# A scan layer on one core: transforms factored 64 by 32 in place of 32 by 64, in eight TensorE tiles at once

## The chip, the core and the metric

The kernel runs on one core of a Trainium2 chip. A core has a matrix engine (TensorE, PE in the profile, whose weight loads stand apart as PEld), three engines for elementwise work (VectorE or DVE, ScalarE or ACT, GpSimd or POOL), and a sync engine (SyncE, SP), which in this kernel only issues DMA transfers. Each engine works through its own list of instructions in order and waits on semaphores for the others. The metric is the device time in microseconds of one execution; three runs of the kernel before gave 559.74, 561.16 and 561.18 us, and the median, 561.16 us, is the time to beat.

## The reference

One sequence of L = 2048 positions with D = 512 channels goes through two branches of the same normalised input, and the result is `x + s * g`:

```
xn = layernorm(x)
dt = exp(log_dt);  logdA = dt * (A_re + i A_im);  dB = dt * B
K[d, l] = real( sum_n C[d,n] * exp(logdA[d,n] * l) * dB[d,n] )     # n: 128 states
y = irfft( rfft(xn, 2L) * rfft(K, 2L) )[:L]                         # per channel
s = y + xn * Dskip
g = silu( gelu(xn @ w1 + b1) @ w2 + b2 )                            # 512 -> 1792 -> 512
out = x + s * g
```

So `s` is a causal convolution of every channel with its own kernel K of 2048 taps, and K has to be computed from the state-space parameters. All is float32.

## The kernel before, in words

The work falls into three stretches of time.

**0 to about 388 us.** Layernorm, the feed-forward branch (each float32 product as three matmuls of a fast format on high and low halves) and the generation of K run together. Their order is written out by hand as a list of tokens, `ORDER`; each token calls one small function. K is generated in 32 pieces (`gen_sum`, L656) and stored to a DRAM buffer `kgd`, 8 pieces for each of the 4 batches of 128 channels (`gen_keep`, L666).

**About 388 to 406 us, the front.** The last matmuls of the feed-forward branch (tokens S and L, `second_part`) alternate with the first transform of batch 0 (`first_dft`, L864). SyncE meanwhile issues the loads of K for batches 0 and 1 (`kernel_load`, L848) and of two tables (`mc` and `tcn`, `table_load`, L798).

**From 406 us on, the batches.** The convolution is done by a transform in factors. The 2048 positions are split as n = N2 n1 + n2, with N1 = 32 and N2 = 64. For each batch, and for K and the signal alike:

- `first_dft` (L864) transforms over n1. Its stationary operand is a group of 32 rows of the data by 128 columns, and its moving operand the table `fc`, 64 columns for real and imaginary parts. 32 such matmuls fill four PSUM banks, each bank from one group of 32 rows, so four of them stand in the array at once. A batch needs four such calls. `first_out` (L870) copies each bank into `X`.
- `second_dft` (L883) applies the twiddle factors and transforms over n2, from the table `mc`, which is stationary in tiles of 64 rows by 64 columns. Real and imaginary parts are two matmuls that accumulate. 32 matmuls fill two banks.
- `spectrum` (L891, ACT) copies the half that belongs to the signal, `product` (L900, DVE) multiplies, and `combine` (L910 and L912, DVE) adds the products into `Y`. Here the sums move between partitions: each is done in two operations on 64 partitions, and its result is laid so that `Y` has 128 rows for the next transform.
- `back_dft` (L918) transforms back over the second factor, with `Y` stationary (128 by 128) and `tcn` moving; `back_out` (L930, ACT) copies into `Z`.
- `swings` (L936, copies L944) transposes `Z` in four quarters; `last_dft` (L975) transforms back over n1 in tiles of 64 rows by 32 columns with 512 moving columns. `last_out` (L982 and L983) multiplies by the gate and adds x, and `store` (L992) writes out. Of the last batch, two quarters go through `rows_out` instead (L1009), whose matmuls have 128 rows.

The order of this part is that of the calls in `slot(b, g)`: a batch b has eight slots g, each with one call of `second_dft`; the even slots also hold a call of `first_dft` for batch b+1, the odd ones a piece of `back_dft` of this batch or the last piece of the batch before, and the transposes and last transforms of batch b-1 stand in between. Two PSUM banks of `second_dft` are double-buffered (tag "ri"); all the other results go round a ring of four banks (`bank`, L804). After the last slot follow the rest of batch 3 and the last stores, from about 540 us.

In the trace one float32 matmul of the program is four records, two weight loads and two matmuls: 1,024 calls at L883 show as 2,048 records of PE and 2,048 of PEld. A transpose, and a matmul of the fast format, is one of each.

Of the kernel before, what the change touches and what calls it, by code (L numbers as in the profile page):

```python
# [25 lines left out]
N1, N2 = 32, 64  # L26
NB = 4
DB = P // NB
# [8 lines left out]
NPH = N1 + N2 // 2  # L37
NPC = 6
NSEED = 11
NREC = 2 + NSEED  # L40
TWO_PI = 6.2831850
# [50 lines left out]
S.28.0 WS.12.0 F.30.1 KL.18.0 E.15.0 WS.12.1 A.17.0 U.13 D S.28.1 F.31.0 KL.17.1 E.15.1 N.16.0 E.15.2  # L92
# [38 lines left out]
def _shape_constants():  # L131
# [3 lines left out]
    cf = np.tile(np.stack([np.cos(a), -np.sin(a)], 1), (G, 1, 1))  # L135
    cg = np.zeros((2, N1, 2, 3, N1))
    for hh in range(2):
        for c, v in enumerate((np.cos(a).T, -np.sin(a).T)):
            cg[hh, :, c, 0] = v
            cg[hh, :, c, 1:].reshape(N1, N1, 2)[:, :, hh] = v  # L140
    cg = cg.reshape(P, 3 * N1)
    n2 = np.arange(N2)[:, None]
    k2 = np.arange(N2)[None, :]
    cm = np.zeros((2, N2, N1, 3, N2))
    ct = np.zeros((2, N2, N1, 2, N2))
    for k in range(N1):
        th = 2 * np.pi * (n2 * (k + 0.25) / L + n2 * k2 / N2)
        c, s = np.cos(th), np.sin(th)
        cm[:, :, k, 0, :] = c
        cm[:, :, k, 1, :] = s  # L150
        cm[:, :, k, 2, :] = -s
        ct[0, :, k, 0, :] = c.T / L
        ct[1, :, k, 0, :] = -s.T / L
        ct[0, :, k, 1, :] = s.T / L
        ct[1, :, k, 1, :] = c.T / L
    ct = ct.reshape(P, N1, 2, 2, 2, 16).transpose(0, 1, 4, 5, 3, 2)
    cb = np.zeros((CH, NPC, CH, NPH))
    for d in range(CH):
        cb[d, :3, d, :N1] = N2 * np.arange(N1)
        cb[d, :3, d, N1:] = np.arange(N2 // 2) + 0.5  # L160
        cb[d, 3:, d, :N1] = 1.0
# [3 lines left out]
        "cg": cg.astype(f),  # L165
        "cm": cm.reshape(P, N1 * 3 * N2).astype(f),
        "ct": ct.reshape(P, N1 * P).astype(f),
# [5 lines left out]
def kernel(  # L173
# [7 lines left out]
    x_t = u[0].rearrange("(n h j t a q) d -> t h a j n q d", n=N1, h=2, j=2, t=2, a=2)  # L181
    o_l = out[0].rearrange("(r j q) d -> j r q d", j=2, q=NQ)
    o_t = out[0].rearrange("(n h j t a q) d -> t h a j n q d", n=N1, h=2, j=2, t=2, a=2)
# [11 lines left out]
    kgd = [dram.tile([P, DB * N2], F32, name=f"kgd{b}") for b in range(NB)]  # L195
# [8 lines left out]
    dsk = keep.tile([P, NB, DB], F32, name="dsk")  # L204
    GP.memset(dsk, 0.0)
    b1s = keep.tile([P, NF], F32, name="b1s")
    fc = keep.tile([P, 2 * N1], F32, name="fc")
# [277 lines left out]
    def params(b):  # L485
# [61 lines left out]
        V.scalar_tensor_tensor(xp[:, 1], ai, (N2 - 1) / 2.0, an, op0=ALU.mult, op1=ALU.add)  # L547
# [63 lines left out]
    def gen_size(s):  # L611
        rc = gen[s]["rc"]
        mm = par.tile([P, CH, N2 + N1], F32, tag="mm", name=f"mm{s}", bufs=2)
        mv = mm.rearrange("p c (j l) -> p c j l", l=N1)
# [5 lines left out]
        GP.tensor_mul(mm[:, :, N1:N2], mm[:, :, 0:N1], rc[:, 12, :].unsqueeze(2).to_broadcast([P, CH, N1]))  # L620
# [10 lines left out]
    def gen_tables(s, n):  # L631
        ra, mm = gen[s]["ra"], gen[s]["mm"]
        m1, m2 = mm[:, :, N2:], mm[:, :, :N2]
        H = N2 // 2
        up = slice(N1, N1 + H)
        dn = slice(N1 + H - 1, N1 - 1, -1)
        if n == 0:
            e1 = par.tile([P, 2, CH, N1], F32, tag="e1", name=f"e1_{s}", bufs=2)
            e2 = par.tile([P, 2, CH, N2], F32, tag="e2", name=f"e2_{s}", bufs=2)
            gen[s]["e"] = (e1, e2)  # L640
            V.tensor_mul(e1, m1.unsqueeze(1).to_broadcast([P, 2, CH, N1]), ra[:, :, :, :N1])  # L641
            return
# [7 lines left out]
    def gen_sum(s):  # L650
        e1, e2 = gen[s]["e"]
        p = pss.tile([P, DD, N2], F32, tag="sm", name=f"kg{s}")
        for d in range(DD):
            for c in range(2):
                for g in range(G):
                    PE.matmul(p[g * N1:(g + 1) * N1, d, :], e1[:, c, g * DD + d, :], e2[:, c, g * DD + d, :],  # L656
                              start=(c == 0), stop=(c == 1), skip_group_check=True)
        gen[s]["p"] = p

    def gen_out(s):  # L660
        gen[s]["ko"] = ko = par.tile([P, DD, N2], F32, tag="ko", name=f"ko{s}", bufs=2)
        A.copy(ko, gen[s]["p"])

    def gen_keep(s):
        b, j = divmod(s, SPB)
        SY.dma_start(kgd[b][:, j * DD * N2:(j + 1) * DD * N2], gen.pop(s)["ko"].rearrange("p a b -> p (a b)"))  # L666
# [62 lines left out]
    def skip_load():  # L729
        for g in range(G):  # L730
            SY.dma_start(dsk[g * N1:g * N1 + 1], dskip.rearrange("(o b g d) -> g o b d", o=1, b=NB, g=G)[g])
        SY.dma_start(fc, cf)

# [38 lines left out]
        "D": skip_load,  # L772
# [10 lines left out]
    def open_front():  # L783
        SB["pf"] = pf = opened(p2, "pf", "right")
        SB["mc"] = pf.tile([P, N1, 3, N2], F32, name="mc")
        SB["psa"] = opened(p2, "psa", "right", bufs=2, space=PSUM)

    def open_mid():
        SB["pm"] = pm = opened(p2, "pm", "right")
        SB["ps"] = opened(pz, "psm", "left", bufs=2, space=PSUM)  # L790
        SB["tcn"] = pm.tile([P, N1, P], F32, name="tcn")
        SB["gc"] = pm.tile([P, N1], F32, name="gc")

    def table_load(t, src):
        w = t.shape[2] if len(t.shape) == 3 else t.shape[2] * t.shape[3]
        for k in range(0, N1, 8):
            d = t[:, k:k + 8]
            SY.dma_start(d.rearrange("p k m -> p (k m)") if len(t.shape) == 3 else d.rearrange("p k a m -> p (k a m)"),  # L798
                         src[:, k * w:(k + 8) * w])
# [12 lines left out]

# [4 lines left out]
    def side_piece(b, g):  # L817
        t = side.setdefault(b, SB.get("raw1"))
        SY.dma_start(t[g * N1:(g + 1) * N1], xs.rearrange("(n m) (b g d) -> b g n m d", n=N1, b=NB, g=G)[b, g])

    def side_load(b):
# [5 lines left out]
        for g in range(G):  # L827
            side_piece(b, g)
# [346 lines left out]
```

## Time and profile before

| what | value |
|---|---|
| median of three runs | 561.16 us (559.74 to 561.18) |
| span of the profiled execution, first to last instruction | 558.0 us |
| granted TensorE clock, mean | 0.998 |
| PE busy | 540.2 us, 97% (7,179 matmul records) |
| PEld busy | 432.1 us, 77% (7,179 records) |
| DVE busy | 454.2 us, 81% (697 instructions) |
| ACT busy | 407.8 us, 73% (602) |
| POOL busy | 296.3 us, 53% (403) |
| DMA | 86.92 MB, mean 156 GB/s |
| instructions in all | 17,143 |

The profiled execution has no run time of its own beside its span; the span lies 3.2 us under the median of the runs, and the profile's shares are shares of the span. PE is busy nearly throughout, and so its share alone does not tell which stretch is bound by what: matmuls are pipelined, their records overlap, and a record is busy from its start to its modelled end. For the stretches it is more useful to see how far apart groups of records start. The table of queues in the profile also lists the transfers that bring the engines' own instructions from memory, as kind "instruction".

### The profile page before, as it was taken

The page shows a single profiled execution, that of the slowest core. Times are in us where ns is not written, and L with a number is a line of the kernel's source. Part 1 is how long each engine was busy: PE and PEld are TensorE (multiplying, and loading weights), DVE is VectorE, ACT ScalarE, POOL GpSimd, SP SyncE. Part 2 cuts the span into 40 slices and gives each one's busy share as a digit, 9 for nine tenths or more (in the row PEclk, how much of TensorE's full clock was granted, in tenths as well). Part 3 has the DMA queues.
Part 4 walks back from the last instruction along what each step waited for, and adds up shares of the span by engine and source line. Part 5 has one row for each costly group of instructions (what it writes and reads, how often), then busy time and mean ns, then how long its engine had stood idle before and what let it go on. Part 6 is the DMA issues. An engine that isn't in the chain of part 4 may idle for free.

```text
span 558.0 us, 17143 instructions
## 1 busy us (share of the span) xinstructions
PE 540.2 (97%) x7179; PEld 432.1 (77%) x7179; DVE 454.2 (81%) x697; ACT 407.8 (73%) x602; POOL 296.3 (53%) x403
## 2 busy tenths in 40 slices
PE   8899999999999999999999999999999999999995
PEld 7567777777777777767777777777889998988872
DVE  6899999999997799988988969877357657767874
ACT  3589997977598999668989798995355565564542
POOL 5639585776966769857718747540320305014323
PEclk9999999999999999999999999999999999999999
DMA  8959337267468392426167049205965583615945
GB/s 188 288 161 311 84 96 210 61 210 228 135 189 269 133 295 81 143 75 192 57 188 219 21 114 186 61 11 181 365 245 79 140 128 95 191 46 127 197 120 113
DMA packets 108345, 86.92 MB, mean 156 GB/s; under 512 B 44294, under 2 KB 87562, under 8 KB 108268
## 3 DMA queue, kind: packets, MB, share of 16 engines
q1 hardware_dynamic: 97584, 65.37, 43.8%
q0 software_dynamic: 9568, 19.93, 12.1%
q8 instruction: 56, 0.92, 0.7%
q10 hardware_dynamic: 1116, 0.53, 0.4%
q14 instruction: 21, 0.17, 0.1%
HBM read 52.25 MB, written 33.55 MB: 154 GB/s over the span
## 4 chain that ended last, share of the span: by engine, by line
PE 68%; DVE 16%; issue 6%; DMA 5%; SPq 2%; ACT 1%; POOL 1%; DVEq 0%; POOLq 0%
PE z L295 8%; PE z L296 7%; PE z L297 7%; PE f L256 7%; PE f L258 7%; PE f L257 7%; PE s L883 6%; PE kg L656 5%; PE s L864 4%; PE sa L918 3%; DMA w2s<-in_B_w_dram 2%; PE ph L595 2%; PE w L936 2%; DVE e L641 2%; DVE hl L282 2%
## 5 line engine op out<-in xcount | busy, mean ns | idle before, releaser
L618 POOL TENSOR_TENSOR mm<-mm,rc 128x32 f32<-128x32 f32 (+4 forms) x150 | 110.7, 738 | 11.8
L295 PE MATMUL z<-w2h,hh 128*128 128x512 f32 x224 | 97.9, 437 | 0.0
L256 PE MATMUL f<-xh,w1h 128*128 128x512 f32 x220 | 92.0, 418 | 0.5 <-ACT hf L270 0.5
L297 PE MATMUL z<-w2h,hl 128*128 128x512 f32 x224 | 88.5, 395 | 0.9 <-DVE hl L282 0.9
L296 PE MATMUL z<-w2l,hh 128*128 128x512 f32 x224 | 88.7, 396 | 0.0
L258 PE MATMUL f<-xh,w1l 128*128 128x512 f32 x220 | 86.9, 395 | 1.5 <-DVE w1l L241 1.5
L257 PE MATMUL f<-xl,w1h 128*128 128x512 f32 x220 | 86.7, 394 | 0.0
L883 PE MATMUL s<-X,mc 64*64 64x128 f32 x2048 | 63.5, 272 | 0.9 <-issue 0.9
L900 DVE TENSOR_TENSOR t<-s,uh 128x512 f32<-128x512 f32 x64 | 41.1, 685 | 25.9 <-ACT uh L891 25.6
L883 PEld LDWEIGHTS s<-X,mc 64*64 64x64 f32 x2048 | 56.0, 133 | 4.8 <-issue 2.7
L641 DVE TENSOR_TENSOR e<-mm,ra 128x1024 f32<-128x1024 f32 x32 | 47.8, 1495 | 4.7 <-POOL mm L618 3.2
L297 PEld LDWEIGHTS z<-w2h,hl 128*128 128x128 f32 x224 | 42.1, 188 | 11.7 <-DVE hl L282 1.8
L258 PEld LDWEIGHTS f<-xh,w1l 128*128 128x128 f32 x220 | 41.3, 188 | 11.9 <-DVE w1l L241 2.1
L615 POOL COPY mm<-rc 128x32 f32<-128x32 f32 x30 | 15.4, 512 | 65.4 <-DVE e L648 49.0
L256 PEld LDWEIGHTS f<-xh,w1h 128*128 128x128 f32 x220 | 41.5, 189 | 10.3 <-ACT hf L270 1.2
L282 DVE TENSOR_TENSOR hl<-hf,hh 128x512 fp32r<-128x512 f32 x56 | 46.7, 838 | 3.4 <-ACT hh L276 3.3
L295 PEld LDWEIGHTS z<-w2h,hh 128*128 128x128 f32 x224 | 42.5, 190 | 9.0
L609 DVE SCALAR_TENSOR_TENSOR ra<-ra,ph 128x512 f32<-128x512 f32 x64 | 43.6, 681 | 6.9 <-ACT ra L603 6.0
L296 PEld LDWEIGHTS z<-w2l,hh 128*128 128x128 f32 x224 | 42.3, 189 | 7.9
L257 PEld LDWEIGHTS f<-xl,w1h 128*128 128x128 f32 x220 | 41.4, 188 | 8.9
L870 ACT COPY X<-s 128x512 f32<-128x512 f32 x56 | 28.9, 598 | 25.6 <-PE s L864 25.6
L645 DVE TENSOR_TENSOR e<-mm,ra 128x1024 f32<-128x1024 f32 x32 | 45.6, 1425 | 0.0
(185 smaller groups left out, 1146.2 us busy)
## 6 DMA issues: line engine op xcount, KB each, us to landing
x<-in_A_u_dram SPq DMA_DIRECT2D x16, 256.0 KB
xs<-x SPq DMA_DIRECT2D x16, 256.0 KB
xt_h<-xh POOLq DMA_DIRECT2D x4, 1024.0 KB, 5.4
xt_l<-xl POOLq DMA_DIRECT2D x4, 1024.0 KB, 7.3
kgd<-ko SPq DMA_DIRECT2D x32, 128.0 KB
za<-zo SPq DMA_DIRECT2D x4, 1024.0 KB
xh<-xt_h POOLq DMA_DIRECT2D x4, 1024.0 KB, 6.8
xl<-xt_l POOLq DMA_DIRECT2D x4, 1024.0 KB, 10.1
```

Of the source, the lines that this page charges most:

```text
L256: PE.matmul(p, wh[:, k, :], xh[:, k, :], start=(k == 0), stop=False)
L257: PE.matmul(p, wh[:, k, :], xl[:, k, :], start=False, stop=False)
L258: PE.matmul(p, wl[:, k, :], xh[:, k, :], start=False, stop=(k == KD - 1))
L282: V.tensor_sub(hl, hf, hh)
L295: PE.matmul(z, hh[:, s], wh, start=(f0 == 0 and not rows), stop=False)
L296: PE.matmul(z, hh[:, s], wl, start=False, stop=False)
L297: PE.matmul(z, hl[:, s], wh, start=False, stop=(f0 == FA - 1))
L609: V.scalar_tensor_tensor(ra[:, 0, c], ra[:, 1, c], MAGIC, p, op0=ALU.subtract, op1=ALU.subtract)
L618: GP.tensor_mul(mv[:, :, 0:3:2, w:2 * w], mv[:, :, 0:3:2, 0:w], rc[:, 2 + 2 * i:4 + 2 * i, :].rearrange("p j c -> p c j").unsqueeze(3).to_ ...
L641: V.tensor_mul(e1, m1.unsqueeze(1).to_broadcast([P, 2, CH, N1]), ra[:, :, :, :N1])
L645: V.tensor_mul(e2[:, :, :, :H], m2[:, :, :H].unsqueeze(1).to_broadcast([P, 2, CH, H]), ra[:, :, :, dn])
L883: PE.matmul(p[ka * 64:(ka + 1) * 64, r, o, :, jj], mc[h, k, ((0, 2), (1, 0))[c][o], :], xf[b][h, c, :, k, :], start=(c == 0), stop=(c == 1 ...
```

## The change

The factors change places: N1 is now 64 and N2 is 32, for the transforms only (the generation of K keeps its 32 by 64 split under the names GA and GB). What follows from it, in the order of the work:

- **first transform** (`first_dft`, L867 of the new file): the stationary operand is now 64 rows by 32 columns of the data, for one x of the batch's positions, and real and imaginary parts are separate matmuls of 64 moving columns. A call has 64 matmuls and fills two banks; a batch has eight calls in place of four, one in every slot.
- **second transform** (`second_dft`, L887): real and imaginary parts stand above one another in the 64 rows of an operand, so nothing accumulates. Its tiles are 64 rows by 32 columns, still 32 matmuls a slot.
- **products** (`combine`): one operation on all 128 partitions for each sum, with no partition moved.
- **back transform** (`back_dft`, L924): two calls a batch, each for half of the frequencies and into all four banks of the ring; 128 matmuls of 32 rows by 64 columns and 64 moving columns a call, pairs of which accumulate. The first call stands at the end of slot 5, the second in slot 1 of the batch after.
- **last transform** (`rows_dft`, L980): for all batches as two matmuls of 128 rows by 64 columns with 512 moving columns a quarter.
- **copies**: the two banks of the first transform go to ACT and DVE in all calls of the front and to ACT alone in the slots; three of the four banks of the back transform go to ACT and one to DVE; of the two copies of each transposed quarter one goes to ACT, one to DVE.
- **loads and stores**: `mc` goes from 3 MB to 2 MB and `tcn` from 2 MB to 1 MB, in fewer transfers; the loads of gate and x and the stores need fewer transfers. The loads of `dsk` and `fc`, which the token D placed in the first stretch, now come after the end of `ORDER`, behind a memset on POOL.

In program order PE's list keeps all of its rows up to the front; behind it the number of float32 matmuls is

| transform | before | after |
|---|---|---|
| first | 512 (L864) | 2,048 (L867) |
| second | 1,024 (L883) | 1,024 (L887) |
| back | 128 (L918) | 1,024 (L924) |
| last | 60 (L975, L1009) | 32 (L980) |

and the transposes stay at 128.

PE's list in batch 0 before, where a second transform is followed by two pieces of the back transform, the next second transform and a first transform of batch 1 (names: `s_0_3` is the second transform of batch 0, slot 3; `sa` the back transform; `s_1_1_0_0` a bank of the first transform of batch 1):

```order
L883 MATMUL s_0_3_5443<-X_5029,mc 64x2x64 x32
L918 MATMUL sa_0_0_5476<-tcn,Y_0_5359 128x128 x4
L918 MATMUL sa_0_1_5481<-tcn,Y_0_5359 128x128 x4
L883 MATMUL s_0_4_5503<-X_5029,mc 64x2x64 x32
L864 MATMUL s_1_1_0_0_5536<-fc,in_1_5021 128x64
L864 MATMUL s_1_1_0_1_5537<-fc,in_1_5021 128x64
L864 MATMUL s_1_1_0_2_5538<-fc,in_1_5021 128x64
L864 MATMUL s_1_1_0_3_5539<-fc,in_1_5021 128x64
```

The last four rows stand eight times over. In the changed program the same part of batch 0 ends slot 5 with a whole half of the back transform:

```order
L867 MATMUL s_1_5_0_6199<-fc,in_1_5021 32x64
L867 MATMUL s_1_5_1_6200<-fc,in_1_5021 32x64
L924 MATMUL sa_0_0_0_6274<-tcn,Y_0_5837 64x64
L924 MATMUL sa_0_0_1_6275<-tcn,Y_0_5837 64x64
L924 MATMUL sa_0_0_2_6276<-tcn,Y_0_5837 64x64
L924 MATMUL sa_0_0_3_6277<-tcn,Y_0_5837 64x64
L887 MATMUL s_0_6_6411<-X_5031,mc 32x2x64 x32
```

Here the two rows of L867 stand 32 times over, and the four of L924 also 32 times, where the list before had eight matmuls of the back transform in a piece.

SP's list, from the last store of the gate in `ORDER` on, before:

```order
L446 DMA gd_69<-zi_4385 128x4x128
L406 DMA zi_5010<-za_73 128x4x512
L666 DMA kgd_85<-ko_4935 128x256
L666 DMA kgd_85<-ko_4980 128x256
L848 DMA in_0_0_4994<-kgd_82 128x1024
L848 DMA in_0_1_4995<-kgd_82 128x1024
L798 DMA mc<-in_cm_dram 128x1536 x4
```

and after:

```order
L441 DMA gd_69<-zi_4377 128x4x128
L661 DMA kgd_85<-ko_4927 256x1x128
L661 DMA kgd_85<-ko_4972 256x1x128
L848 DMA in_0_0_4986<-kgd_82 64x1024 x2
L848 DMA in_0_1_4987<-kgd_82 64x1024 x2
L789 DMA dsk<-in_A_Dskip_dram 1x4x64 x2
L790 DMA fc<-in_cf_dram 128x128
L401 DMA zi_5010<-za_73 128x4x512
L796 DMA mc<-in_cm_dram 128x1024 x4
```

`fc`, which every first transform reads, is now loaded behind the two last stores of K and the four loads of K for batch 0; the load of `zi`, the stored half of the feed-forward result, comes behind it.

The core of the diff:

```diff
-N1, N2 = 32, 64
+N1, N2 = 64, 32
+GA, GB = 32, 64
...
-        ps = [bank(f"s1_{b}_{u}_{h}_{g}").rearrange("p e (i m) -> p (e i) m", m=N2) for g in gs]
+        ps = [bank(f"s1_{b}_{n}_{g}").rearrange("p e (i m) -> p (e i) m", m=N1) for g in range(GU)]
         for i in range(8):
-            for g, p in zip(gs, ps):
-                r = slice(g * N1, (g + 1) * N1)
-                PE.matmul(p[:, i, :], src[r, 2 * i:2 * i + 2, :], fc[r], start=True, stop=True, skip_group_check=True)
+            for c in range(2):
+                for x in range(2):
+                    for g, p in enumerate(ps):
+                        r, o = slice(g * N1, (g + 1) * N1), (2 * x + c) * N2
+                        PE.matmul(p[o:o + N2, i, :], src[r, 16 * s + 2 * i + x, :], SB["fc"][r, c], start=True, stop=True,
+                                  skip_group_check=True)
...
-                for c in range(2):
-                    for ka in range(2):
-                        for r in range(2):
-                            k, h = 4 * g + 2 * jj + ka, slice(r * 64, (r + 1) * 64)
-                            PE.matmul(p[ka * 64:(ka + 1) * 64, r, o, :, jj], mc[h, k, ((0, 2), (1, 0))[c][o], :],
-                                      xf[b][h, c, :, k, :], start=(c == 0), stop=(c == 1), skip_group_check=True)
+                for ka in range(KA):
+                    for r in range(2):
+                        k, h = KM * ka + 2 * g + jj, slice(r * 64, (r + 1) * 64)
+                        PE.matmul(p[ka * N2:(ka + 1) * N2, r, o, :, jj], mc[h, k, o, :], xf[b][h, :, k, :], start=True, stop=True,
+                                  skip_group_check=True)
...
-        for ka in range(2):
-            r = slice(ka * 64, ka * 64 + 64)
-            if c == 0:
-                eng.tensor_sub(Y[0:64, ka, :, js], t[r, 0, :, js], w[r, 1, :, js])
-            else:
-                eng.tensor_add(Y[64:128, ka, :, js], t[r, 1, :, js], w[r, 0, :, js])
+        if c == 0:
+            eng.tensor_sub(Y, t[:, 0, :, js], w[:, 1, :, js])
+        else:
+            eng.tensor_add(Y, t[:, 1, :, js], w[:, 0, :, js])
...
-        for e in range(4):
-            PE.matmul(p[:, e, :], Y[:, 4 * h + e, :], SB["tcn"][:, 8 * j + 4 * h + e, :], start=True, stop=True)
+        for m in ms:
+            for c in range(2):
+                for r in range(2):
+                    for a, p in enumerate(ps):
+                        q = slice(a * N2, (a + 1) * N2)
+                        PE.matmul(p[r * DB:(r + 1) * DB, m], Y[q, c, m, r, :], SB["tcn"][q, c, 8 * h + m, :], start=(c == 0), stop=(c == 1),
+                                  skip_group_check=True)
...
+        second_dft(b, g)
+        ys = {3: 0, 4: 1, 6: 2, 7: 3}
+        if b and g in ys:
+            rows_dft(b - 1, ys[g])
+        if nxt:
+            first_dft(b + 1, g)
+        spectrum(b, g)
+        if nxt:
+            first_out(b + 1, g)
+        if b and g == 1:
+            back_dft(b - 1, 1)
+            back_out(b - 1, 1, (A, V, A, A))
+        product(b, g)
+        if g % 2:
+            combine(b, g // 2, 1, V)
+            combine(b, g // 2, 0, V)
+        if b and g in ys:
+            rows_out(b - 1, ys[g])
+        sw = {2: 0, 3: 1, 4: 2, 6: 3}
+        if b and g in sw:
+            swings(b - 1, sw[g], None, (A, V))
+        if g == 5:
+            back_dft(b, 0)
+            back_out(b, 0, (A, V, A, A))
...
     with tc.manual_schedule():
         SB["spare"] = False
         open_front()
+        skip_load()
         z_load(NTB - 1)
...
+        for q4 in range(4):
+            swings(b, q4, None, (A, V))
+        for q4 in range(4):
+            rows_dft(b, q4)
+            rows_out(b, q4, V, (SY, A))
```

More of the change, by code (lines that the diff above doesn't have):

```diff
@@ L194 @@
     pcd = [dram.tile([P, NPC * NS], BF16, name=f"pcd{b}") for b in range(NB)]
-    kgd = [dram.tile([P, DB * N2], F32, name=f"kgd{b}") for b in range(NB)]
+    kgd = [dram.tile([G * GA, 2, SPB, DD * N2], F32, name=f"kgd{b}") for b in range(NB)]
     keep = ctx.enter_context(tc.tile_pool(name="keep", bufs=1, side="left"))
@@ L826, in side_load @@
         side[b] = t
-        for g in range(G):
-            side_piece(b, g)
+        for n in range(2 * GU):
+            side_piece(b, n)
     def side_turn(b):
@@ L846, in kernel_load @@
             k = [wka.tile([P, DB // 2, N2], F32, tag="x", name=f"in1_0_{h}", bufs=2) for h in range(2)]
+        rows = kgd[b].rearrange("(g h a) i s e -> h g (a i) (s e)", g=GU, h=2)
         for h in range(2):
-            SY.dma_start(k[h], kgd[b].rearrange("p (h d m) -> p h d m", h=2, m=N2)[:, h])
+            for g in range(GU):
+                SY.dma_start(k[h][g * N1:(g + 1) * N1].rearrange("p d m -> p (d m)"), rows[h, g])
         side[b].append(k)
```

321 lines of the change are left out of this document (114 added, 207 removed).

## The prediction

> **What bounds the kernel now.** I read the busy table by stretches first, because an average over 558 us hides that the stretches differ. Columns: the stretch, its length, then busy us and records of PE, PEld, DVE, ACT and POOL, the granted clock, the DMA share and GB/s.
>
> ```profile
> 0.00:388.00 388.00, 379.82 (x3563) 292.95 (x3563) 344.11 (x532) 321.61 (x446) 251.73 (x353) 1.00 0.55 156
> 388.00:418.00 30.00, 29.15 (x658) 24.79 (x650) 13.12 (x21) 13.03 (x23) 7.91 (x10) 1.00 0.81 302
> 418.00:540.00 122.00, 121.01 (x2908) 108.60 (x2908) 87.93 (x131) 68.92 (x127) 31.61 (x36) 1.00 0.59 128
> 540.00:558.00 18.00, 10.27 (x84) 5.79 (x68) 9.03 (x16) 4.21 (x8) 5.03 (x4) 0.94 0.41 89
> ```
>
> The change leaves PE's list up to 388 us as it is. From 418 to 540 us PE is busy 121.0 of 122 us, DVE 87.9, ACT 68.9: PE sets the pace there. The chain of waits in the middle of a batch has PE's groups back to back:
>
> ```profile
> 444.35 1.91 PE s L883 x64
> 446.26 1.94 PE s L864 x64
> 457.79 1.91 PE s L883 x64
> 459.70 1.02 PE y L975 x16
> 460.72 1.98 PE sa L918 x16
> ```
>
> So a second transform (32 matmuls, 64 matmul records) costs 1.91 us, a first transform of 32 matmuls 1.94, two pieces of the back transform 1.98, and eight matmuls of 64 by 32 tiles and 512 columns, eight tiles at once, 1.02.
>
> The next view is what decides my forecast. The timeline of PE around the front shows short stops that no semaphore ends (releaser "issue"):
>
> ```profile
> 401.77 2.60 PE L864 MATMUL s<-fc,in 32*128 32x64 f32 x64
> 405.89 1.96 PE L883 MATMUL s<-X,mc 64*64 64x128 f32 x58
> 408.15 0.44 PE L883 MATMUL s<-X,mc 64*64 64x128 f32 x6 [0.30 <-issue]
> 408.52 2.01 PE L864 MATMUL s<-fc,in 32*128 32x64 f32 x64
> 410.47 1.96 PE L883 MATMUL s<-X,mc 64*64 64x128 f32 x58
> 412.98 2.19 PE L883 MATMUL s<-X,mc 64*64 64x128 f32 x70 [0.55 <-issue]
> 415.10 2.15 PE L864 MATMUL s<-fc,in 32*128 32x64 f32 x64
> ```
>
> From the resumption at 408.15 to the one at 412.98 lie 6 + 64 + 58 = 128 matmul records, and with a weight load for each, 256 instructions. The table of queues says what 256 is:
>
> ```profile
> span 558.0 us, 17143 instructions
> q8 instruction: 56, 0.92, 0.7%
> q14 instruction: 21, 0.17, 0.1%
> ```
>
> (packets, MB, share of 16 engines.) 0.92 MB in 56 packets is 16,400 B a packet; 0.92 + 0.17 MB over 17,143 instructions is 64 B each; so a packet holds 256 instructions, and 56 of them are 14,336, PE's 2 x 7,179 = 14,358. PE reads its program in pages of 256 instructions, and at both stops the page was late. How late a page can be, I read from the DMA table of short windows. The first row is that of 410.4 to 411.6 us, the second of 412.98 to 414.2, the third of 418 to 540:
>
> ```profile
> q8 instruction: 1, 0.02, 5.4%
> q8 instruction: 1, 0.02, 6.2%
> q8 instruction: 23, 0.38, 1.4%
> ```
>
> A window of 412.98 to 414.1 has no such packet, so the page after the one entered at 412.98 begins to arrive 1.1 us after the entry. It takes 1.4% x 16 x 122 / 23 = 1.19 us (5.4% x 16 x 1.2 = 1.04 for the first). The one that ended before 411.6 released PE at 412.98, 1.4 us later. Added up: 1.1 + 1.2 + 1.45 = **3.8 us a page**, if the request for a page goes out only when the one before it is entered. The stops bear that out: entries at 401.9 (inside the 2.60 us group of 401.77), 408.15, 412.98 and, where the group of 415.10 is 0.2 us too long, 416.9, are 6.2, 4.8 and 3.9 us apart, the longer ones while the tables are loaded (DMA share 0.81). If several pages were held ahead, PE would not have stopped at 408.15 after a stretch of feed-forward matmuls that takes few instructions. From 418 to 540 us before, 5,816 records are 22.7 pages in 122 us, 5.4 us each: the 3.8 us were covered there.
>
> **The change part by part.** *Instructions.* A float32 matmul is two weight loads and two matmuls in the trace:
>
> ```profile
> L883 PE MATMUL s<-X,mc 64*64 64x128 f32 x2048 | 63.5, 272 | 0.9 <-issue 0.9
> L883 PEld LDWEIGHTS s<-X,mc 64*64 64x64 f32 x2048 | 56.0, 133 | 4.8 <-issue 2.7
> ```
>
> for 1,024 calls, and a transpose one of each. From the first transform of batch 0 on, the new list has: front 8 x 64 x 4 = 2,048, and 42 for seven feed-forward parts; batch 0 8 x 128 (second) + 8 x 256 (first) + 512 (back) = 3,584; batches 1 and 2 1,024 + 2,048 + 1,024 + 64 (transposes) + 32 (last) = 4,192 each; batch 3 1,024 + 1,024 + 96 = 2,144; the rest 608. That is 16,810, or 65.7 pages; half of one is in hand when it begins: 65.2 periods. At 3.8 us they need about 248 us, where the stretch before, from 391.8 to the last add at 553.3, took 162.
>
> *PE's own work* shrinks. The generator's matmuls show tiles of 64 columns, four at a time (first row; the other rows serve this and the terms below):
>
> ```profile
> 384.48 1.10 PE L656 MATMUL kg<-e,e 128*32 128x64 f32 x64
> 452.19 1.75 PE w L936 x16
> 550.24 0.69 DVE L1011 TENSOR_TENSOR last<-y,last 128x512 f32<-128x512 f32 x1 [0.79 <-PE y L1009]
> 552.62 0.69 DVE L1012 TENSOR_TENSOR last<-last 128x512 f32<-128x512 f32 x1
> L900 DVE TENSOR_TENSOR t<-s,uh 128x512 f32<-128x512 f32 x64 | 41.1, 685 | 25.9 <-ACT uh L891 25.6
> L912 DVE TENSOR_TENSOR Y<-t,t 64x512 f32<-64x512 f32 x30 | 23.5, 784 | 0.7
> L662 ACT COPY ko<-kg 128x256 f32<-128x256 f32 x32 | 11.8, 368 | 4.8 <-PE kg L656 4.8
> 391.84 2.01 PE L864 MATMUL s<-fc,in 32*128 32x64 f32 x64
> ```
>
> 64 records in 1.10 us at four tiles make 128 records in 1.1 at eight: a call of the first transform. A back half is 256 records, 2.2 us. A second transform, 1.91 at four tiles, takes 1.0 at eight. In sum 32 x 1.0 + 24 x 1.1 + 8 x 2.2 + 128 x 1.75 / 16 (transposes) + 16 x 1.04 (last) = 106 us, against 121 now. If the eight tiles ran only four at a time, PE's work would be some 180 us, still under the 236 that the pages need: this unknown costs nothing here, the pages cover it. If the cover is gone, the 106 counts (rival 1).
>
> *First call late.* SP before:
>
> ```profile
> 386.05 2.96 SPq L666 DMA_DIRECT2D kgd<-ko  x2
> 389.06 1.79 SPq L848 DMA_DIRECT2D in<-kgd  x2
> 390.95 1.99 SPq L798 DMA_DIRECT2D mc<-in_cm_dram  x4
> ```
>
> `fc` now stands behind four loads of K and two of `dsk`: six issues of 0.5 (as `mc`) to 0.9 us (as `in`) from 389.06 put it at 392.1 to 394.5, and it needs some 2 us to land. The first transform before began at 391.84. PE waits in order, the feed-forward parts behind it. `dsk` waits besides for a memset on POOL, which has little to do there (7.9 of 30 us). 0 to +6 us, I take **+3**, so 395.
>
> *Copies and products.* DVE loses eight operations of 0.73 us a batch and gains six copies; ACT loses six copies. The copy of K to `ko` becomes strided: at most 0.69 for 0.37 us, 32 times, under a PE that is busy 379.8 of 388 us. Fewer and shorter transfers. All at 0: the pages of batches 0 to 2 leave 8 us a slot, and a slot has two products (1.37), a sum (0.7) and one or two copies.
>
> *Where the pages do not set the pace*: in batch 3 a slot has 140 instructions on the mean without the back transforms, 0.55 page or 2.1 us, but DVE has two products of 0.685, a sum, and in every second slot a gate product and a copy, about 3.0 us: 8 x 0.9 = 7. At the end, four quarters of gate product and add (0.69 + 0.86) follow the last matmuls' copies, 8 us against 1.4 of pages: 7. Together **+14**. The last add ends at 553.3 now and the span 4.7 us later; I keep **4.7**.
>
> Sum: 395 + 14.9 (the first three periods, in the same burst of table loads) + 62.2 x 3.8 = 236.4 + 14 + 4.7 = 665.0 us of span; the runs lie 3.2 above it: **668 us**. Ends: with 3.4 us a page (a short transfer of 1.04, and each of the gaps 0.1 shorter) 62.2 x 0.4 = 25 less, 643; with 4.6 us, just under the loaded period of 4.8, 50 more, 718; the call of `fc` moves either by 3.
>
> The Trainium skill, "Runtime: NRT & Kernel Launch", section "Instruction fetch mechanics", says that an engine's instructions come in blocks of 16 KiB, 256 of them, that the next page is fetched while the current one runs, and that the cost of crossing a block is mostly hidden. The trace agrees with the block; with "hidden" it agrees from 418 to 540 us and not at 408.15 and 412.98. By that rule alone the pages would cost nothing and the first rival below would hold.
>
> **The rivals.**
>
> 1. *The pages stay hidden and the smaller work of PE shows: faster.* This ends on the other side. It decides if PE may go through a page in under 3.8 us, with further pages held ahead. Then from about 409 (the front's 406 and the late `fc`) come 106 us of matmuls and some 27 of waits (a back half waits for all four banks of the ring, the last transform for its copies, about 5 us a batch, and the 7 at the end): 409 + 133 + 4.7 = 546.7, **550 us**. For it: 3.8 us were covered throughout the batches before. Against: the stops at exactly 256 instructions, and the missing packet between 411.6 and 414.1.
> 2. *A page takes two thirds of it or less*, because two requests can be under way when PE runs dry, or because the 1.1 us before a packet is idle time that a hungry PE does not see. At 2.5 us: 395 + 65.2 x 2.5 = 163, + 14 + 4.7 = 576.7, **580 us**. For it: no stretch before runs through more than two pages dry. Against: 1.2 us of transfer and 1.45 us after it already make 2.6.
> 3. *No change*: at 2.2 us a page the sum is 395 + 143 + 14 + 4.7 + 3.2 = **560 us**. Any period near it on either side gives another verdict, so it needs a coincidence.
>
> **How the numbers follow.** Forecast 0.84, rival 1 0.08, rival 2 0.06, no change 0.02. Everything but rivals 1 and 3 is slower: 0.90; faster by over 0.3% (about what a measurement of this kernel can tell) 0.08; within 0.3% 0.02. The range is that of the forecast with the two ends of the page's period and of the first call, drawn down towards rival 2: 628 to 718.
>
> **What would show it.** PE and PEld records rise from 7,179 to about 12,000 each, and q8 from 56 packets to some 94. In the timeline of the batches PE runs 128 matmul records in 1 to 2 us and then stops with the releaser "issue", the entries 3.8 us apart; a slot of batch 1 takes near 7.8 us, and a first transform with its second, 384 instructions, 5.7 us. PE's busy share from 418 us on falls to half or less, DVE's and ACT's too. The packets' share of 16 engines rises while other DMA falls. I am wrong if q8 packets come less than 3 us apart, or if groups of 256 records pass in 1 to 2 us without a stop; the first call of the first transform later than 401 us or not later than 392 would put the term of `fc` wrong; and a stretch after the last page of more than 25 us the term of 14.

## The result and the profile after

The changed kernel takes 698.47 us (median of four runs, 694.14 to 703.51) against 560.7 us; the ratio is 1.2457, 95% interval 1.2387 to 1.2527. The forecast was 668 us, with 628 to 718 as its range.

The page of the changed kernel: span, PE's rows, the granted clock in 40 slices, and the transfers of instructions:

```profile
span 692.3 us, 26606 instructions
PE 572.9 (83%) x11983; PEld 444.6 (64%) x11983; DVE 445.6 (64%) x685; ACT 395.8 (57%) x579; POOL 290.5 (42%) x395
PEclk9999999999999999999999959877778686875867
q8 instruction: 94, 1.54, 1.0%
```

PE's records are 11,983 of each kind and the packets 94, as counted beforehand. The busy table by stretches (columns as before):

```profile
0.00:388.00 388.00, 379.72 (x3563) 293.18 (x3563) 344.45 (x532) 321.56 (x446) 251.06 (x353) 1.00 0.55 155
388.00:420.00 32.00, 19.95 (x675) 14.89 (x669) 3.90 (x7) 2.96 (x6) 4.84 (x6) 0.68 0.69 206
420.00:660.00 240.00, 154.18 (x7357) 123.69 (x7363) 82.33 (x125) 65.93 (x119) 32.05 (x34) 0.78 0.34 72
```

Up to 388 us nothing has changed: all of the loss lies behind. There no engine is full any more: from 420 to 660 us PE is busy for 64% of the time, where it was 99% in the batches before, DVE for 34%, ACT for 27%. The granted clock, 1.00 before, is 0.78.

The groups of PE's records over the whole span say where PE stands still (behind the second bar: idle us just before them, and what ended it):

```profile
L867 PE MATMUL s<-fc,in 64*32 64x64 f32 x4096 | 61.5, 252 | 52.0 <-issue 46.5
L924 PE MATMUL sa<-tcn,Y 32*64 32x64 f32 x2048 | 39.6, 307 | 35.1 <-issue 30.8
L887 PE MATMUL s<-X,mc 64*32 64x128 f32 x2048 | 52.1, 331 | 13.3 <-issue 7.4
```

85 us of idle end with "issue", that is, with no semaphore that the profile shows. PE's timeline at the start shows both what ends there and how long it takes:

```profile
391.37 0.40 PE L292 MATMUL z<-w2h,hl 128*128 128x512 f32 x1
396.63 2.05 PE L867 MATMUL s<-fc,in 64*32 64x64 f32 x128 [4.86 <-DMA fc<-in_cf_dram]
...
400.19 1.39 PE L867 MATMUL s<-fc,in 64*32 64x64 f32 x78
403.68 1.06 PE L867 MATMUL s<-fc,in 64*32 64x64 f32 x50 [2.10 <-issue]
...
406.24 1.35 PE L867 MATMUL s<-fc,in 64*32 64x64 f32 x75
412.06 1.09 PE L867 MATMUL s<-fc,in 64*32 64x64 f32 x53 [4.47 <-issue]
```

The first transform of batch 0 waits 4.9 us for the table `fc`, and then PE stops in the middle of a call, with nothing in the profile that it waits for: 50 records, 3 feed-forward matmuls and 75 records lie between two stops, 128 weight loads and 128 matmuls.

How the pages follow one another, from the table of DMA queues in three windows that each begin at a packet (401.2 to 416.5 us, 416.5 to 619.85, 619.85 to 679.2):

```profile
q8 instruction: 3, 0.05, 1.3%
q8 instruction: 51, 0.84, 1.8%
q8 instruction: 11, 0.18, 1.3%
```

So 15.3 us for three periods in the front, 203.4 for 51 (3.99 us each) in batches 0 to 2, and 59.3 for 11 (5.39 each) from the start of batch 3.

### The profile page after: what moved, and what is told of

Same layout as the page of the kernel before. It is cut to its first block, busy times and chain, and to the rows that moved or that the text cites. A ratio compares the mean times of both kernels' runs of the same rounds, so it can differ in the third digit from the quotient of the medians.

```text
span 692.3 us, 26606 instructions
## 1 busy us (share of the span) xinstructions
PE 572.9 (83%) x11983; PEld 444.6 (64%) x11983; DVE 445.6 (64%) x685; ACT 395.8 (57%) x579; POOL 290.5 (42%) x395
## 5 line engine op out<-in xcount | busy, mean ns | idle before, releaser
L867 PE MATMUL s<-fc,in 64*32 64x64 f32 x4096 | 61.5, 252 | 52.0 <-issue 46.5
L867 PEld LDWEIGHTS s<-fc,in 64*32 64x32 f32 x4096 | 52.9, 118 | 68.0 <-issue 61.2
L924 PE MATMUL sa<-tcn,Y 32*64 32x64 f32 x2048 | 39.6, 307 | 35.1 <-issue 30.8
L887 PE MATMUL s<-X,mc 64*32 64x128 f32 x2048 | 52.1, 331 | 13.3 <-issue 7.4
L986 POOL TENSOR_TENSOR xb<-gb,xb 128x512 f32<-128x512 f32 x10 | 12.8, 1277 | 117.7 <-DVE gb L985 117.7
L924 PEld LDWEIGHTS sa<-tcn,Y 32*64 32x64 f32 x2048 | 34.6, 192 | 40.8 <-issue 34.7
L935 DVE COPY Z<-sa 128x512 f32<-128x512 f32 x9 | 6.1, 690 | 83.4 <-PE sa L924 83.4
L887 PEld LDWEIGHTS s<-X,mc 64*32 64x32 f32 x2048 | 38.6, 126 | 20.3 <-issue 14.5
L636 DVE TENSOR_TENSOR e<-mm,ra 128x1024 f32<-128x1024 f32 x32 | 47.7, 1491 | 4.8 <-POOL mm L613 3.3
L935 ACT COPY Z<-sa 128x512 f32<-128x512 f32 x23 | 12.0, 593 | 67.5 <-PE sa L924 67.5
```

The lines of the kernel that those rows point to most:

```text
L636: V.tensor_mul(e1, m1.unsqueeze(1).to_broadcast([P, 2, CH, GA]), ra[:, :, :, :GA])
L867: PE.matmul(p[o:o + N2, i, :], src[r, 16 * s + 2 * i + x, :], SB["fc"][r, c], start=True, stop=True, skip_group_check=True)
L887: PE.matmul(p[ka * N2:(ka + 1) * N2, r, o, :, jj], mc[h, k, o, :], xf[b][h, :, k, :], start=True, stop=True, skip_group_check=True)
L924: PE.matmul(p[r * DB:(r + 1) * DB, m], Y[q, c, m, r, :], SB["tcn"][q, c, 8 * h + m, :], start=(c == 0), stop=(c == 1), skip_group_check=True)
```

## The experiments

Each run is on the kernel named, compared with the kernel before on the same chip; the times are medians. The changed kernel's 698.5 us is the one measurement of the result, whose runs lie between 694.1 and 703.5, so a few microseconds of any difference to it mean nothing.

| run | PE instructions against its base | time, us | base, us |
|---|---|---|---|
| pairs | changed, -4,096 (16 pages) | 646.3 | 698.5 |
| eighths | changed, -7,168 (28) | 619.3 | 698.5 |
| few | changed, -9,216 (36) | 592.6 | 698.5 |
| twice the streaming | changed, 0 | 697.9 | 698.5 |
| back in 128 columns | changed, -2,048 (8) | 681.8 | 698.5 |
| without loads | changed, 0 | 675.6 | 698.5 |
| `fc` by ACT's queue | changed, 0 | 694.1 | 698.5 |
| split, two orders | before, +4,096 (16) | 606.5, 608.5 | 561.0, 561.4 |
| tail | before, +4,096 (16) | 612.6 | 561.4 |

The theory was the prediction's: PE gets its program one page of 256 instructions ahead, a page costs some 3.8 us, and the change has too many instructions for its work. The rivals: the matrix work itself (small tiles, a lowered clock), and copies and waits for banks.

### Fewer instructions for the same streaming

```diff
-        for i in range(8):
+        for i in range(0, 8, 2):
...
-                        PE.matmul(p[o:o + N2, i, :], src[r, 16 * s + 2 * i + x, :], SB["fc"][r, c], ...)
+                        PE.matmul(p[o:o + N2, i:i + 2, :], src[r, 16 * s + 2 * i + x, :],
+                                  SB["fc"][r, c:c + 1].to_broadcast([N1, 2, N1]), ...)
```

> The changed kernel, but the first transform computes only every second position of a bank and streams the table for it twice (one matmul of 128 moving columns in place of two of 64): same columns streamed, same banks filled, same copies, 4,096 PE instructions fewer, 16.0 pages of 256; every second column of the first transform holds its neighbour's value. Theory (PE waits for its own program, one page ahead): in the changed kernel instruction packets start 4.28 us apart on the mean, so 16 x 4.28 = 68 us less, about 630 us; q8 packets 94 -> 78. Rival A (64 by 32 tiles do not run together, or the matrix work at the lowered clock of 0.75 sets the pace): streaming is unchanged and only weight loads go, at most 12 us less, 687 to 698. Rival B (copies out of the banks and waits for the ring set the pace): unchanged, 698.

Measured: 646.29 us, 52 less, and 78 packets. Rivals A and B allowed 12 and 0. But a page gave 3.3 us, not 4.28, and the time is 16 us above the 630 expected.

The same with 8 in place of 2:

> As the run with pairs, but one position of eight is computed and its table streamed eight times (one matmul of 512 columns): 7,168 PE instructions fewer, 28 pages; the other seven columns hold its value. Theory: 28 x 4.28 = 120 us less, about 579 us, q8 packets 66, and the gain per page is the same as with pairs. Rival A: at most 20 us less. Rival B: 698.

619.25 us, 79 less for 28 pages, 2.8 us each: 40 us short of the expectation. Two things were wrong in it. The mean of 4.28 us contains delays behind data transfers (below), which do not go away with a page. And the pages that are left are no longer the only bound: PE's idle with releaser "issue" from 420 us on, added over its groups, fell from 77.5 us in the changed kernel to 55.2 with pairs and 37.4 here, 28.0 of them in the back transform, which is still spread over two pages a call.

```profile
L924 PE MATMUL sa<-tcn,Y 32*64 32x64 f32 x2048 | 33.0, 252 | 33.4 <-issue 28.0 <-ACT X L875 2.9 <-DVE spare L985 2.5
```

Then the back transform as well:

```diff
-                for r in range(2):
-                    for a, p in enumerate(ps):
-                        PE.matmul(p[r * DB:(r + 1) * DB, m], Y[q, c, m, r, :], SB["tcn"][q, c, 8 * h + m, :], ...)
+                for a, p in enumerate(ps):
+                    PE.matmul(p[:, m], Y[q, c, m].rearrange("p r x -> p (r x)"), SB["tcn"][q, c, 8 * h + m, :], ...)
```

> The run with eighths, and besides the back transform as matmuls of 32 rows by 128 columns (both halves of the stationary operand at once, which alone leaves the result as it is): 2,048 instructions fewer again, 36 pages in all. This is the changed kernel nearly without its pages. Theory: the pages no longer set the pace everywhere, matrix work and waits for copies do; 550 to 565 us (by pages alone 545), PE busy over 85% from 420 us on, clock back to 1.0. If the change had a second loss of its own (a new wait, the lost concurrency), the time stays above 580.

592.56 us. With 17,390 instructions, about as many as the kernel before has (17,143), and with seven eighths of the first transform's results left out, the new form is still 33 us slower than the kernel before. By the expectation a time above 580 means a second loss. The timeline of this run shows a part of it, at full clock:

```profile
472.16 4.27 PE L923 MATMUL sa<-tcn,Y 32*128 32x64 f32 x124 [0.33 <-ACT X L875]
476.36 1.32 PE L887 MATMUL s<-X,mc 64*32 64x128 f32 x64
477.61 1.08 PE L979 MATMUL y<-bs,gc 128*64 128x512 f32 x4
```

PE runs nearly without a stop here, and a back half takes 4.3 us and more. The changed kernel's own form of it, with 256 records a half, is quicker, though dearer than the 2.2 us that I had given it. At full clock it can be seen in the run with eighths:

```profile
530.73 3.13 PE L924 MATMUL sa<-tcn,Y 32*64 32x64 f32 x249 [0.16 <-ACT X L875]
```

So a half of this form is some 3.2 us, and some 8 us of the second loss, 1 a half, come from the edit itself. In the changed kernel the back transform mostly runs at a lowered clock: the last of the following rows stands in a stretch where the granted clock is 0.50, the four before it in one where it is 1.00.

```profile
549.57 1.09 PE L941 MATMUL w<-ident,Z 128*128 128x128 f32 x8
550.59 1.16 PE L887 MATMUL s<-X,mc 64*32 64x128 f32 x64
551.68 1.08 PE L980 MATMUL y<-bs,gc 128*64 128x512 f32 x4
552.68 1.48 PE L867 MATMUL s<-fc,in 64*32 64x64 f32 x128
569.14 2.25 PE L924 MATMUL sa<-tcn,Y 32*64 32x64 f32 x128 [3.62 <-issue]
```

Adding PE's work up again at full clock: 32 x 1.16 (second) + 24 x 1.48 (first) + 8 x 3.2 (back) + 16 x 1.09 (transposes of a quarter) + 16 x 1.08 (last) = 133 us. The same sum for the kernel before, from the prediction's rows, is 32 x 1.91 + 12 x 1.94 + 16 x 1.98 + 14 + 7 x 1.02 + 2.4 = 140. So the change saves PE some 7 us by these rows, where the prediction had 106 us for the new form. The 33 us are not accounted for by this alone; the run also keeps the wait for `fc` (5 us), 11.7 us of stops with releaser "issue", and waits for copies, and how much each of them adds was not taken apart.

### More streaming for the same instructions

```diff
+            w = min(2, 8 - i)
...
-                        PE.matmul(p[o:o + N2, i, :], src[r, 16 * s + 2 * i + x, :], SB["fc"][r, c], ...)
+                        PE.matmul(p[o:o + N2, i:i + w, :], src[r, 16 * s + 2 * i + x, :],
+                                  SB["fc"][r, c:c + 1].to_broadcast([N1, w, N1]), ...)
```

> The changed kernel with the same instructions, but each matmul of the first transform (save the last of a bank row) streams 128 columns, the second 64 of which the next matmul overwrites: nearly twice the streaming of this transform, result unchanged. Theory: the pages cover it, 698 us within 1%, and the idle of PE with releaser issue shrinks by what the matmuls grow. Rival A (matrix work at a lowered clock): 32 calls of about 1.1 us more at full clock, some 2 at half: 730 to 760 us.

697.89 us. PE's work grows, 1.48 us to 1.92 for a call at full clock, and the time does not move; PE's matmuls fill stops that were there:

```profile
419.56 1.92 PE L868 MATMUL s<-fc,in 64*32 64x128 f32 x128
422.30 1.17 PE L868 MATMUL s<-fc,in 64*32 64x128 f32 x65
424.05 1.04 PE L868 MATMUL s<-fc,in 64*32 64x128 f32 x63 [0.59 <-issue]
```

Rival A falls here for the first transform: neither its small tiles nor the lowered clock sets its pace. The other transforms were not tried in this way.

### The back transform alone

The edit of the run with few instructions, without that of the first transform.

> The changed kernel with the back transform as 64 matmuls of 32 rows by 128 columns a call in place of 128 of 32 by 64: both halves of the stationary operand at once, same result, 2,048 PE instructions or 8.0 pages fewer. In the run with few instructions such a half took 4.27 us, in the changed kernel 128 records of the old form 2.25 and a half 4.5: matrix work alike. Theory: 8 pages at 3.3 us (what the run with pairs gave a page) to 3.75 us (the period of quiet pages) less, 668 to 672 us. Rival (what counts is the number of copies, waits or matrix work): no change, 698.

681.83 us (ratio to the kernel before 1.218, 1.2104 to 1.2256), 17 less for 8 pages; 26 to 30 were expected. The direction is that of the theory, the size is not. The expectation took the matrix work of the two forms for alike, from a row of 2.25 us at a granted clock of 0.50 and one of 4.27 at 1.00; at full clock a half is 3.2 us in the old form. The rows of the new one:

```profile
562.17 7.11 PE L923 MATMUL sa<-tcn,Y 32*128 32x64 f32 x128 [3.52 <-issue]
637.67 3.80 PE L923 MATMUL sa<-tcn,Y 32*128 32x64 f32 x128
```

A half is now one page, and that page's own work takes 3.8 us at full clock and up to 7.1 where the granted clock is 0.50. A page costs the longer of the two, its work or its arrival; two pages at 3.7 have become one at 4 to 7. Here the lowered clock costs time; in the changed kernel a page of the back transform takes 2.25 us at 0.50, less than its page needs to arrive.

### The same instructions in the kernel before

```diff
-                            PE.matmul(p[ka * 64:(ka + 1) * 64, r, o, :, jj], mc[h, k, ((0, 2), (1, 0))[c][o], :],
-                                      xf[b][h, c, :, k, :], start=(c == 0), stop=(c == 1), ...)
+                            for v in range(2):
+                                PE.matmul(p[ka * 64:(ka + 1) * 64, r, o, v, jj], mc[h, k, ((0, 2), (1, 0))[c][o], :],
+                                          xf[b][h, c, v, k, :], start=(c == 0), stop=(c == 1), ...)
```

> The kernel before with each matmul of its second transform split into two of 64 moving columns: result unchanged, 4,096 PE instructions or 16.0 pages more, same streamed columns. Theory: from 418 to 540 us it has then some 38 pages; at 3.75 us and some 20 us of late packets behind data transfers 160 us in place of 122, so 590 to 605 us, and stops after each 256 instructions as in the changed kernel. Rival (pages are free unless the tables are being loaded): 128 records of 64 columns four at a time take 2.2 us (as the generator's) in place of 1.91, 32 x 0.3 = 10 us more, 571.

606.46 us, ratio 1.0829 (1.077 to 1.0889), just above the expectation. In this order the sum of one half is still open when that of the other begins in the same bank, and the second transform's sums come out changed by it, against what was expected; so the split was run again with each sum closed first (`v` outside `c`):

> The split of the second transform once more, on the kernel before, with the two matmuls of a sum next to one another, so that one half of a bank is closed before the other is opened: 4,096 PE instructions more as in the first split, result unchanged. Theory: the order does not matter, 600 to 612 us as the first split; rival (the first split was slow because two sums were open in one bank): 565 to 575.

608.48 us, and the result is unchanged. Its timeline shows the kernel before with the changed kernel's stops, 4,096 instructions richer and otherwise the same:

```profile
496.83 2.10 PE L883 MATMUL s<-X,mc 64*64 64x64 f32 x128
501.59 3.18 PE L864 MATMUL s<-fc,in 32*128 32x64 f32 x64 [2.66 <-issue]
504.70 3.69 PE L883 MATMUL s<-X,mc 64*64 64x64 f32 x128
```

A split transform takes 2.1 us of PE in place of 1.91, 6 us over 32 of them at full clock; 47 were lost. Of these, 23 us stand in the profile as stops with releaser "issue". PE's rows behind 405 us are some 27 us longer in all, those 6 among them, at a granted clock of 0.90 from 405 to 590 us, and this run does not tell what the lowered clock cost by itself.

### The price of a page by itself

```diff
+        for w in (64, 8):
+            ps = [bank(f"tail{w}_{g}").rearrange("p e (i m) -> p (e i) m", m=64) for g in range(2)]
+            for _ in range(16):
+                for i in range(4):
+                    for o in range(0, P, 32):
+                        for g, p in enumerate(ps):
+                            r = slice(g * 64, (g + 1) * 64)
+                            PE.matmul(p[o:o + 32, i, :w], ident[r, o:o + 32], fc[r, :w], ...)
```

> The price of a page by itself: the kernel before, followed at its end, where no transfer but the last stores runs, by 512 float32 matmuls in 64 by 32 tiles with 64 moving columns and then 512 with 8, whose results nobody reads: 2,048 instructions, 8.0 pages, of each kind. Theory: PE goes through 256 instructions in 3.5 to 3.9 us whatever they do, 16 pages in 56 to 62 us, about 614 to 620 us in all, and stops after every 128 matmul records. Rival (a page is late only where transfers are in its way): 16 x 1.5 = 24 us and less for the short ones, 575 to 585 us.

612.56 us, 51 more and a little under the 614 expected (the first of the matmuls run beside the last stores). PE's timeline from its first stop to its last; eleven rows like those shown are left out:

```profile
557.22 2.04 PE L1152 MATMUL tail<-fc,ident 64*32 64x64 f32 x128 [2.62 <-issue]
560.95 2.04 PE L1152 MATMUL tail<-fc,ident 64*32 64x64 f32 x128 [1.70 <-issue]
...
583.13 1.37 PE L1152 MATMUL tail<-fc,ident 64*32 64x8 f32 x128 [1.88 <-issue]
...
608.79 1.00 PE L1152 MATMUL tail<-fc,ident 64*32 64x8 f32 x85 [2.37 <-issue]
```

Every page holds 128 matmul records, and 14 of them take 608.79 - 557.22 = 51.6 us: **3.68 us each**, the same for 2.04 us of work as for 1.37. The matmuls are shorter, the stops longer. In each of the 14 periods the packet of the next page begins 1.0 to 1.2 us after PE resumes, takes 0.9 to 1.5, and PE resumes 1.2 to 1.5 after its end: the three parts of the prediction (1.1, 1.2 and 1.45), each seen 14 times. The busy table for this stretch has the DMA at a share of 0.03, the granted clock (the third number from the end) at 0.50, and the other engines idle:

```profile
557.00:609.00 52.00, 23.94 (x1821) 21.94 (x1825) 0.00 (x0) 0.00 (x0) 0.00 (x0) 0.50 0.03 8
```

So neither contention nor another engine makes this price.

### What makes a page dearer than that

```diff
-        q.dma_start(t[0], gd[b].rearrange("p (q m) -> p q m", m=P)[:, n])
-        for j in range(2):
-            q.dma_start(t[1][j * 64:(j + 1) * 64], x_l[j, :, n, cs])
+        GP.memset(t[0], 1.0)
+        GP.memset(t[1], 0.0)
```

(and likewise the loads of the signal and of K for batches 2 and 3; the output is no longer the layer's).

> The changed kernel without most transfers of the batches: gate and x of the last steps, and the signal and K of batches 2 and 3, are memsets on POOL instead of loads (so the output is not the layer's); stores stay. Instructions of PE are the same. In the changed kernel packets start 3.4 to 4.1 us apart where DMA is idle and 4.5 to 8 us where a load fills the queues; the excess over 3.75 us sums to some 24 us from 420 to 660 us. Theory with contention (a page waits behind data in the DMA engines): 670 to 680 us, periods 3.4 to 4.1 us nearly throughout. Theory without (late pages have another reason, such as PE's low clock): 695 to 700, long periods remain.

675.63 us (ratio 1.2073, 1.2037 to 1.2109): 23 us less, as expected of contention. From 420 to 660 us, the changed kernel first and the run without loads second:

```profile
DMA packets 23743, 17.25 MB, mean 72 GB/s; under 512 B 9600, under 2 KB 20864, under 8 KB 23680
```

```profile
DMA packets 6913, 5.23 MB, mean 22 GB/s; under 512 B 448, under 2 KB 6592, under 8 KB 6848
```

The periods of the pages in the run without loads, counted as in the result (windows 417.03 to 610.84 us and 610.84 to 660.2, each from a packet to a packet):

```profile
q8 instruction: 51, 0.84, 1.8%
q8 instruction: 11, 0.18, 1.5%
```

The same 51 periods take 193.8 us in place of 203.4, 3.80 each, and the 11 behind them 49.4 in place of 59.3: the two gains, 9.6 and 9.9, are all of the 18.9 us by which the profiled span is shorter (673.4 against 692.3).

One place in the changed kernel, PE's timeline:

```profile
457.78 0.42 PE L887 MATMUL s<-X,mc 64*32 64x128 f32 x8 [2.27 <-issue]
...
457.99 1.54 PE L867 MATMUL s<-fc,in 64*32 64x64 f32 x117
463.62 0.33 PE L867 MATMUL s<-fc,in 64*32 64x64 f32 x10 [4.09 <-issue]
```

PE enters a page at 457.78, and the next is there 5.8 us later; its packet begins at 460.6. In between, from 457.78 to 460.6, the only traffic is a load of the signal in pieces of 256 bytes, which fills the engines, and no instruction packet:

```profile
DMA packets 2086, 0.53 MB, mean 187 GB/s; under 512 B 2086, under 2 KB 2086, under 8 KB 2086
q1 hardware_dynamic: 2086, 0.53, 127.1%
```

(transfers that run side by side are added, hence over 100%). The trace does not show what a packet waits for; with the run without loads beside it, the reading is that a page stands behind data that has been queued before it.

### The late table

```diff
-        SY.dma_start(SB["fc"].rearrange("p c k -> p (c k)"), cf)
+        A.dma_start(SB["fc"].rearrange("p c k -> p (c k)"), cf)
```

> The changed kernel with the load of the table fc issued from ACT's queue in place of SP's, where it stood behind six others. In the changed kernel the first transform starts at 396.6 us, 4.9 us after PE is free. Theory: the late load moves all that follows, as the pages behind it come one by one: 3 to 5 us less, 693.5 to 695.5, and PE waits at most 1 us there. Rival: the pages of the front are late by themselves behind the table loads, so the gain is taken back: 698.

694.08 us (687.61 to 696.35), 4.4 less than the changed kernel, within the expectation, but with runs that spread by more than this, so that a gain is not shown. The wait is gone, and the page behind it is now late in the table loads:

```profile
391.63 1.67 PE L867 MATMUL s<-fc,in 64*32 64x64 f32 x128
...
394.12 1.02 PE L867 MATMUL s<-fc,in 64*32 64x64 f32 x78
397.59 0.74 PE L867 MATMUL s<-fc,in 64*32 64x64 f32 x50 [2.45 <-issue]
```

No run of the changed form comes near the kernel before, the quickest of them being 33 us slower with part of its results left out. Nothing here points to a version that beats it: by the rows at full clock PE's own work is 133 us against 140.

## Why the prediction was right, and where it was not

- **Cause.** Pages of 256 instructions, fetched one ahead, set the pace from the first transform on. The runs with fewer instructions in the changed kernel and with more in the kernel before, the one with twice the streaming, and the stops after each 128 records show it. The Trainium skill's "mostly hidden" ("Runtime: NRT & Kernel Launch", section "Instruction fetch mechanics") held for the batches of the kernel before and does not hold here, where 85 us of stops are seen.
- **Number of pages.** 94 packets and 11,983 records, as counted.
- **Price of a page.** Added up as 3.8 us from one packet, its gap before and its gap after; measured alone 3.68. Rival 2 (2.5 us, two requests under way) falls with that, and rival 3 with it.
- **What was undersized** is the use of this quiet price for all 62 pages. Batches 0 to 2 took 3.99 us a page: 51 x 0.19 = 10 us more. Behind them the sum has 11.2 x 3.8 + 14 + 4.7 = 61.3 us; measured are 692.3 - 619.85 = 72.4, 11 more. I had kept the loaded period for the upper end only. The run without loads puts some 19.5 of these 21 us on data transfers: there the 51 periods are 3.80 us each, the prediction's price. Its last 11 periods, 49.4 us, are still 7 or 8 above 11 x 3.8, about what the sum has for the slots of batch 3.
- **The front.** The first transform began at 396.6 us, not 395: SP issued the load of `fc` at 393.25, within the range given, but the table took 3.4 us from there, not 2. PE entered the next page 81 records into this transform, at 397.8, and the packet of the page behind it began 3.5 us later, not 1.1. From the start of the transform to this packet, at 401.2, are 4.6 us for which the sum, which counts its periods from 395, has nothing: together some 6 us. The three periods that followed came to 15.3, taken as 14.9, and that is luck: the first was 8.1 us and the others 3.7 and 3.4, against 6.2, 4.8 and 3.9.
- **Run against span.** The median lies 6.2 us above the span, not 3.2; the profiled execution was the quickest of the four. The 10, the 11 and the 6 above are the 27 us by which the span is longer than the sum; this 3 makes up the 30 between 668 and 698.
- **PE's own work** was the wrong step of the working: 106 us by eight tiles at once, and 133 by rows at full clock, most of the difference in the first transform (1.48 for 1.1 a call) and the back transform (3.2 for 2.2 a half). It is no term of the sum, since the pages cover it, and cost the forecast nothing. It carried rival 1, though: with 133 in place of 106 that rival's own sum gives an estimate of 577 us, not 550, and no gain. That slower tiles would cost nothing here held where it was tried, with twice the streaming in the first transform.
- **Costs put at nothing** in the first stretch (the strided copy of K, smaller transfers) hold: it takes the same 388 us.
- **Told wrongly of the profile:** PE's busy share was to fall to half or less, and is 64%; records are counted to their modelled ends and stretch at a lower clock.

## What to carry to other kernels

Count instructions of TensorE, not only columns: a float32 matmul is four of them here, and 64 matmuls are a page, which takes 3.7 us to arrive and more behind data transfers. Work cut into tiles so small that 64 matmuls run in under 3.7 us left the array idle in the runs here, however many tiles stood in it at once. To see it in a profile, look for stops with releaser "issue" in the middle of a group and count records between two of them; where 128 pairs lie between, fewer and longer matmuls helped here, and so did keeping data transfers out of the way; more or fewer columns a matmul changed nothing while the page took longer.

## What was not expected of the hardware

- A page's price was about the same at two granted clocks: 3.68 us in the tail run at 0.50, and 3.8 by the rows of the kernel before at 1.00. In the changed kernel the clock fell to 0.78 as PE stood still, and twice the streaming of the first transform cost nothing.
- Tiles a quarter or an eighth of the array do not run faster in proportion. At full clock 128 records, each with its weight load, take 2.10 us as 64 by 64 tiles with 64 columns, 1.48 as 64 by 32 tiles with 64 columns, and 1.92 with 128 columns; as 32 by 64 tiles 249 records take 3.13 us, about 1.6 for 128, and as 32 by 128 tiles 124 take 4.27. Halving the columns streamed saves a quarter, and halving the width of a stationary operand of 32 rows from 128 to 64 more than half.
- 2,086 pieces of 256 bytes, 0.53 MB of data, hold up a page for 1.7 us beyond the usual gap, though they come from another queue.
